# Start-up order, norm rows and value phases of a gated attention and spectral mix

## The chip, the cores and the metric

The kernel runs on one core of a Trainium2 chip. The metric is device time in microseconds for one execution: the median of three runs. One further execution is profiled, and its own time is given beside its span, which goes from the first to the last instruction.

## The reference

Two branches read the same kind of input and a sigmoid gate mixes them, row by row. Branch A is full attention with 16 heads of 28 columns over 2048 positions; branch B is a 2-D real Fourier transform, a multiplication by complex weights and the inverse transform.

```
g = sigmoid((A_x * gate_w).sum(-1))
qkv = (A_x @ wqkv)            # [2048, 448] @ [448, 1344]
p = softmax(q @ k.T * 28**-0.5)      # 16 heads, 2048 x 2048
a = (p @ v) @ wo
b = irfft2(rfft2(B_x) * (B_w_r + 1j * B_w_i))
return g * a + (1 - g) * b
```

In the kernel both branches read A_x.

## The kernel before

**Tiling.** The 16 heads form four groups of four heads; a head takes 32 rows (28 and some spare) of a 128-row tile, so that one group fills `q[g]` and `k[g]`, each [128, 2048]. Queries are taken in four blocks of 512. A *round* n is one group and one query block: 16 rounds. A round has 16 key tiles of 128 keys; a *unit* is one key tile and one head, 128 keys by 512 queries.

**Two ways of making exponentials.** For most units ScalarE makes them from PSUM: a *step* is three units (buffer `psA`, 1536 columns) or two (`psB`, 1024 columns) in turn, one instruction at L944, and the result goes to the SBUF ring. There are 331 steps. The last `ND[n]` key tiles of a round (49 in all) go another way: the score of one unit goes to a background bank `bg`, VectorE (L979, 196 times) adds a constant and writes it as a 16-bit integer whose bits are a rough exponential in bf16; then three more copies with shifted *phase* are made by VectorE or GpSimd (L990, 147 in all), each of 128x2048. The four phases are averaged by the accumulation: `vd[g]` holds the values multiplied by a weight for each phase.

**Norm rows.** The queries and keys have a spare row in each head with minus half the squared norm, which keeps the exponent in range. A row is made from squares (`sq`) and a small matmul with a constant (`cst`). `proj_group` (L690) makes it apart: project, evacuate to `k` or `q` (L710, L712), square (L716), matmul, evacuate to `nrow` (L731), and a DMA on SP's queue puts it into its rows. `proj_two` (L744), used for key block 1 of group 0, projects twice: once to get the squares, and once into a PSUM bank onto which the norm matmul then accumulates. The factor e^(..) that the key's norm takes away is put back by `w` (`w_block`, L776, exponentials at L806) into the values.

**Values.** `v_block` (L817) projects four key tiles' values into one bank; VectorE multiplies them by `w` into `vw` (L846), and for the last block of a group by four weights `wg` into the four phases of `vd` (L856), straight from PSUM.

**Head.** `head` (L496) starts the loads: x tiles and constants on SP's queue; on ScalarE's queue the query weights, the identity matrix, the key weights, in this order. Fourteen matmuls of zeros warm TensorE. x is transposed by TensorE into `psA`, `psB`, `pvb` and a background bank. Block 0 of the queries is projected twice (into `psA` for the squares, into `pvb` for the result with its norm row), and so are the first 128 keys; the other 384 keys of block 0 follow. `weights` loads the rest, `x_block` (L665) transposes the later x blocks.

**Spectral branch.** `background` gives the transforms as matmuls (`Bd`, `A`, `CS`, `Binv`) with DMA shuffles between them (`Ab`, `V2`), spread as background work over the whole kernel. `out_tile` adds both branches into PSUM (eight groups of matmuls for each of 16 row tiles).

**Order.** Every piece of work is an `Op` with an engine, a duration and dependences. The order in which they are issued is not worked out at run time: `PLAN` holds a list of op numbers, made beforehand, the background bank of each item, and the list of phases that VectorE rather than GpSimd makes. `issue` (L296) emits them in that order, and each engine runs its own instructions in order. Codes from 60000 in the list are fillers: small matmuls of zeros into the accumulator or a background bank. All matmuls in groups of four (one for each 32 rows or columns) come from L414, transposes from L422. Where a GpSimd op follows a VectorE op marked `lk`, `issue` adds a dependence between them.

```
for (n, kt, s) in st:
    deps += self.qev[g, c] + ([self.k0] if (g, kt) == (0, 0) else self.kev[g, kt // 4])
```

A score step waits for its queries (`qev`) and keys (`kev`; `k0` is the first 128 keys).

Of the kernel before, what the change touches and what calls it, by code (L numbers as in the profile page):

```python
# [39 lines left out]
TWO = (1,)  # L40
EARLY = 8
PLAN = (
    (
        'c-kFTW3XU7)0~-TCTDHiwr$(IYukF(wr$(CZQHtQd-uEF`y*9JD$}P=cPFV3SO9Pk6$Byxf`Vw^AtD429U_5-7!VE&M248q6=FdR'
        'V5kd~AU4#5dQc1EKz)b{wV@(3fOrrB%^*HBf(p<a8bbnT0pTGbG=Y|o2wFo2NDOVDBP4~kkOVqGJBR|QAUULj6wnz`Lr+K#-Jmk0'
        'fn?ANGC*4B4(T8>WP#q06?#B6$OwHP6ZC}wkR5WsK*$d{Ar}mT+>i(ILOv)6qoEKKh9Xb~N<&d71~VZom4#U_8`4p6C;=s*3Y3C!'
        'FbB%RTu4tDDFe-e`LF;M!VcI8yI>LQhD?;1_P}CT0!twa?S-tg4E8}b+7GMY0A#0wupCyvN>~FqXcer5LvR?@!4b$wM<Ewofva!~'
        'a?>@q4#(jp+=AP11M<)v$V+$O1mvUqbQ12teRu$;;2{*Cg7gR`Kp|QWkD)M4grc+oCczUZLK|T+td}Y96sE#7C`QkqI8BEcun9K9'
        '7T5|Us3dKJ?Qk0I*i!TrO4B#^4prd?oPn}bhR#AY_zCCWJZz8)@C(Y(MJP{~;4(aiyY@G{fQnRss>4h81EIhu_zFD!g-R4)9jHv<'
        'uqnKTH}Do3LKUh?@1Pa@gKG3106#!`s7@aNu?rC1v!5Uy)ubBq8SdK$_M!a(k8CY^Y!%j~{Su!Jh{l6*ND@#TN=S9-xIQdT>{DBh'  # L50
        'PUwifJ|&_^KC+ME6H^0fNKySW``jj>O%g&$sS#b!o8_Y3B3tE!ZA{yw34N3A@<W<ZGWsda=!{NIzvQJ2wJGSV-XqN^CAFZv^2(+n'
        'gDvT`ZAGc+ptiVAzS?j0kaoT`Ic!7Wk^LJhzAbs*j?U@8f44vEc^v`UQwNHOhxHNNk&fy}*oltmpZ1at2|X3oI#U<AtWRp~tm{g@'
        'Y&T+eU2e!t=}uR454t5+wQ)U3TravUzpZ!I^groMedx3f6WOOB@_os<esohSAGm(-$KKL^?SJ$i^r!3kt-Y=L!#jIJzqbQuAl=db'
        '>;Sl{2SG^a8Mzn6U@#1#!88QU3b_0FxqPrg=!FcWNBW$+l*c+$KH6av68cIW=;8ECf3oO4+vobcjGzlr*pH-(Qp8`9$oNo4!BJGy'
        'kEY8K6^r?3IEKg-_t9}IJ<(sRa!+*$9|L3JI11;+Q%N5SW8+YmKuKL34DTk=3!Tip)XCj&NZ}^Y2$)Robf}KuMnX*YUcc5U-4q%H'
        'Q|XN!1F76wJr+LbaWIXhQv~->f70V2qKoAsxz9R{n?Z4LCcV<}Fg||K32+w8roTENe$|m(Y?s<aadRlG`={s9PaW08aldplm(CrR'
        '6Ecs!>G||spOhc^lq{h1ZXul(W#YQ%P8(wu(PFYDp3CB$Swc%Gs~5v2gUjYaLcIwIO@xVY8D;m&DV#}yIebzK%nFL{R#Hx%48xoI'
# [188 lines left out]
class Kernel:  # L246
# [249 lines left out]
    def head(self):  # L496
# [9 lines left out]
        for i, (w, off) in enumerate((("q", 0), ("k", D))):  # L506
# [3 lines left out]
            if i == 0:  # L510
                d_id = self.dma(self.ident[:], ident.ap(), (), K0 + 1, eng="ACT", dur=0.43, lat=2.4)
# [52 lines left out]
        def proj(w, bank, a, b, last, key, deps=(), **it):  # L564
            ops = []
            for j, c in enumerate(CO):
# [5 lines left out]
                if it and it["first"] and ops:  # L572
                    d["first"] = False
# [769 lines left out]
```

## Time and profile before

| what | value |
|---|---|
| runs | 406.08 us median of 3 (405.11 to 407.94) |
| profiled execution | 405.44 us, span 403.6 us |
| TensorE (PE) busy | 390.3 us, 97%, 5099 matmuls |
| ScalarE (ACT) busy | 382.9 us, 95%, 350 instructions |
| VectorE (DVE) busy | 326.2 us, 81%, 527 |
| GpSimd (POOL) busy | 160.0 us, 40%, 190 |
| DMA | 21.69 MB, mean 54 GB/s |

Busy times are unions of instruction spans. Matmul spans overlap their successors and include their drain, so a TensorE that is 97% busy is not at its peak; where it matters the distance between starts is used. The first exponential starts at 12.34 us, the last at 392.70 us. In the timeline's rows the first number is the start in us, the second the duration in us (with x and a count: of the whole group), then engine, line, operation, output <- input and shape; in brackets the idle time of that engine just before, and what ended it. In rows that group instructions the numbers behind the bar are total busy time in us and mean time of one in ns, or min/median/max in ns.

### The profile page before, as it was taken

Reading aid. Unit: us, or ns where it says so; the run is one execution under the profiler, and the core shown is the slowest. Engines: PE = TensorE matmul, PEld = TensorE weight load, DVE = VectorE, ACT = ScalarE, POOL = GpSimd, SP = SyncE. Lnnn points to the kernel's source line nnn. Section 1 sums busy time; section 2 is a strip of 40 time slices with the busy share of each in tenths; the row PEclk is TensorE's granted clock in tenths of the full one; section 3 lists DMA queues with packets and bytes.
Section 4 is the critical chain, followed back from the end, with each engine's and each line's share of the span. In section 5 each row is a group of like instructions: output and inputs, shape, how many; then the busy total and the mean of one; then the engine's idle time right before and its main releaser. Section 6 shows DMA issues by size and latency. Waiting matters only on the chain.

```text
span 403.6 us, 12270 instructions
## 1 busy us (share of the span) xinstructions
PE 390.3 (97%) x5099; PEld 147.3 (36%) x5099; DVE 326.2 (81%) x527; ACT 382.9 (95%) x350; POOL 160.0 (40%) x190
## 2 busy tenths in 40 slices
PE   7999999999999999999999999899999999999996
PEld 5544333233343343323433333334333433333333
DVE  1456798997687999997899989899999998776733
ACT  3799999999989999999999999999999999999992
POOL 7004013531303332555345466561655557215230
PEclk9999999999999999999999999999999999999999
DMA  8014032220101011201222232323012201011011
GB/s 222 3 43 99 4 89 61 51 65 16 51 15 39 7 37 51 71 25 46 71 71 56 55 91 51 78 54 75 31 36 79 83 24 52 25 52 36 26 52 58
DMA packets 31995, 21.69 MB, mean 54 GB/s; under 512 B 16736, under 2 KB 29780, under 8 KB 31940
## 3 DMA queue, kind: packets, MB, share of 16 engines
q1 hardware_dynamic: 30580, 20.45, 18.8%
q8 instruction: 40, 0.66, 0.7%
q10 hardware_dynamic: 1360, 0.46, 0.4%
q14 instruction: 15, 0.12, 0.1%
HBM read 15.00 MB, written 1.97 MB: 42 GB/s over the span
## 4 chain that ended last, share of the span: by engine, by line
PE 65%; ACT 14%; DVE 11%; issue 5%; DMA 3%; POOL 2%; SPq 0%; ACTq 0%; DVEq 0%; POOLq 0%
PE bg L414 27%; PE pvb L414 19%; ACT ring L944 14%; PE psA L414 10%; PE psB L414 8%; DVE pd L979 4%; DVE pd L990 2%; POOL pd L990 2%; DMA ident<-cident 1%; DMA CS<-cCS 1%; DVE pvs L1058 1%; DVE X L1275 1%; DMA Rb<-rsc 1%; DVE tt L1232 1%; PE bg L422 1%
## 5 line engine op out<-in xcount | busy, mean ns | idle before, releaser
L944 ACT ACTIVATE ring<-psA 128x1536 bf16<-128x1536 f32 x162 | 247.6, 1529 | 1.6 <-PE psA L414 1.3
L944 ACT ACTIVATE ring<-psB 128x1024 bf16<-128x1024 f32 x161 | 178.3, 1107 | 3.3 <-PE psB L414 2.1
L979 DVE TENSOR_SCALAR pd<-bg 128x512 uint16<-128x512 f32 x196 | 130.0, 684 | 19.4 <-PE bg L414 17.1
L990 POOL TENSOR_SCALAR pd<-pd 128x2048 uint16<-128x2048 uint16 x56 | 105.6, 1897 | 90.5 <-DVE pd L990 31.1
L414 PEld LDWEIGHTS <-k 32*128 32x128 bf16 x1024 | 40.0, 91 | 111.7 <-issue 105.4
L414 PE MATMUL pvb<-ring,vw 128*32 128x512 bf16 x808 | 74.8, 384 | 0.3 <-DVE pvs L1058 0.3
L414 PE MATMUL bg<-q,k 32*128 32x512 bf16 x196 | 72.5, 381 | 0.5 <-DVE nrow L731 0.2
L414 PE MATMUL pvb<-pd,vd 128*32 128x512 bf16 x784 | 69.4, 384 | 1.8 <-DVE pvs L1058 0.8
L990 DVE TENSOR_SCALAR pd<-pd 128x2048 uint16<-128x2048 uint16 x91 | 69.5, 791 | 0.8
L414 PE MATMUL psA<-q,k 32*128 32x512 bf16 x498 | 65.8, 383 | 2.6 <-ACT ring L944 1.4
L414 PE MATMUL psB<-q,k 32*128 32x512 bf16 x330 | 66.8, 383 | 0.5 <-DVE k L613 0.2
L1069 POOL TENSOR_TENSOR q<-pvs,Rb 128x512 bf16<-128x512 f32 x15 | 19.6, 1304 | 41.8 <-DMA Rb<-rsc 32.1
L414 PEld LDWEIGHTS <-vw 128*32 128x32 bf16 x828 | 20.2, 94 | 33.9 <-issue 29.7
L414 PEld LDWEIGHTS <-vd 128*32 128x32 bf16 x784 | 20.3, 94 | 32.7 <-issue 26.9
L414 PEld LDWEIGHTS <-xT 112*128 112x128 bf16 (+1 forms) x512 | 18.9, 97 | 13.2 <-issue 10.3
L1062 POOL TENSOR_TENSOR rrg<-rr,G 128x16 f32<-128x16 f32 x15 | 3.3, 218 | 49.3 <-DVE rr L1061 37.7
L414 PE MATMUL bg<-xT,wpk 112*32 112x512 bf16 (+3 forms) x268 | 21.2, 380 | 0.1
L1232 DVE TENSOR_TENSOR tt<-bg,Wg 128x900 bf16<-128x900 f32 x16 | 17.4, 1093 | 2.9 <-PE bg L414 2.6
L414 PE MATMUL bg<-xT,wpq 112*32 112x512 bf16 (+1 forms) x240 | 18.0, 383 | 0.0
L414 PE MATMUL bg<-Bd,xT 112*32 112x450 bf16 x256 | 17.3, 357 | 0.0
L712 DVE TENSOR_SCALAR q<-bg 128x512 bf16<-128x512 f32 x15 | 10.3, 688 | 7.3 <-PE bg L414 7.3
L414 PE MATMUL pvb<-zero 128*32 128x256 bf16 x260 | 15.7, 276 | 0.2 <-DVE pvs L1058 0.2
(112 smaller groups left out, 341.9 us busy)
## 6 DMA issues: line engine op xcount, KB each, us to landing
Rb<-rsc SPq DMA_DIRECT2D x60, 64.0 KB
CS<-cCS SPq DMA_DIRECT2D x16, 192.0 KB
xtok<-Ab SPq DMA_DIRECT2D x16, 112.5 KB
Wg<-in_B_w_i_dram SPq DMA_DIRECT2D x64, 28.1 KB
V<-xtok SPq DMA_DIRECT2D x16, 112.5 KB
xtok<-in_A_x_dram SPq DMA_DIRECT2D x3, 448.0 KB
out_dram<-fin SPq DMA_DIRECT2D x12, 112.0 KB
Wg<-in_B_w_r_dram SPq DMA_DIRECT2D x32, 28.1 KB
```

What stands on the lines that cost most here:

```text
L414: self.pin(self.nc.tensor.matmul(out, lhsT=lhsT, rhs=rhs, start=start, stop=stop, **kw))
L422: self.pin(self.nc.tensor.transpose(out=out, in_=in_, identity=self.ident[0:n, 0:n]))
L712: self.pin(nc.vector.tensor_scalar(out=dst, in0=self.bgi(it), scalar1=CQ, scalar2=None, op0=ALU.mult))
L944: self.pin(nc.scalar.activation(out=home[:, u0:u0 + len(st), :], in_=slot[:, 0:len(st), :], func=ACT.Exp, scale=LN2 / UNITS))
L979: self.pin(nc.vector.tensor_scalar(out=self.pd[y.bank][:, s, :].bitcast(U16), in0=self.bgi(it), scalar1=127 * UNITS, scalar2=0.0, op0=ALU. ...
L990: self.pin(e.tensor_scalar(out=fl(self.pd[z.bank]), in0=fl(self.pd[y.bank]), scalar1=float(PHASE[f]), scalar2=1.0, op0=ALU.add, op1=ALU.mult))
L1058: ev = self.dve(0.6, lambda: self.pin(nc.vector.tensor_copy(out=pvs[:], in_=self.pv[:])), last + [self.nlast[i]], -1000.0, name="evac")
L1062: b = self.pool(0.2, lambda: self.pin(nc.gpsimd.tensor_tensor(out=rrg[:], in0=rr[:], in1=self.G4[:, c, :], op=ALU.mult)), [a] + self.g4d, ...
L1069: e = self.pool(1.24, lambda: self.pin(nc.gpsimd.tensor_tensor(out=dst, in0=pvs[:], in1=self.Rb[:], op=ALU.mult)), ds, kk)
L1232: self.pin(nc.vector.tensor_tensor(out=tt[:], in0=free_dims(self.bgi(it), [[0, 2], [F, 2], [1, F]]), in1=free_dims(Wg[:], [[F, 2], [F, 2], ...
L1275: self.pin(nc.vector.tensor_tensor(out=free_dims(self.zt[0:FN], [[128, 4], [1, 128]], 512 * t), in0=self.bgi(it)[0:FN, :].rearrange("p (a ...
```

## The change

- On ScalarE's queue the identity is loaded first, then the query weights, then the key weights.
- The start of group 0: the second query projection goes. VectorE scales the query from `psA` into `q`, a matmul puts the norm row alone into `pvb`, and VectorE adds the two. The first part of the keys is 256 instead of 128 columns (`KA`), and the squares of the rest are made by VectorE instead of ScalarE. The first half of x block 1 is transposed in the head; its second half uses `pvb`.
- `proj_add` takes the place of `proj_two` (key block 1) and of `proj_group` for the other blocks of group 0 (key blocks 2 and 3, query blocks 1 to 3): one projection, evacuated at once; its square; a matmul of the norm row into a second bank; and a VectorE instruction that adds it. The `nrow` copy and the DMA go.
- `v_block`: VectorE copies the values to a float tile `vraw`, and GpSimd makes the four phases of `vd` from it.
- Within a quad of the VectorE way, the four scores wait for the first score of the previous quad instead of its last.
- `w` has two buffers instead of four.
- A new `PLAN`: 2959 entries instead of 2964, 68 fillers instead of 66, 85 phases on VectorE instead of 91 (so 62 instead of 56 on GpSimd).

```diff
+KA = 256
...
             if i == 0:
-                d_id = self.dma(self.ident[:], ident.ap(), (), K0 + 1, eng="ACT", dur=0.43, lat=2.4)
+                d_id = self.dma(self.ident[:], ident.ap(), (), K0, eng="ACT", dur=0.43, lat=2.4)
+            raws[w] = self.dma(free_dims(self.U[0:C], [[C, 4], [1, C]], o), self.wsrc(off, 0, C), (), K0 + 1 + i,
+                               eng="ACT", dur=0.55, lat=3.0)
...
-        qb = proj("q", bqb, 0, 512, False, K0 + 22, [self.xev[0, 2], ka])
-        kb = proj("k", bkb, 0, 128, False, K0 + 23, [self.xev[0, 1], qb])
+        kb = proj("k", bkb, 0, KA, False, K0 + 22, [self.xev[0, 2], ka])
...
+        mq = self.pe(0.227, lambda: self.mm(bqb(), self.c("selq"), self.sq[:, 0:512], True, True),
+                     (sqq, self.d_cst, self.xev[0, 1]), K0 + 21)
...
+        qc = self.dve(0.6, lambda: self.pin(nc.vector.tensor_scalar(out=q0[:, 0:512], in0=bqa(), scalar1=CQ, scalar2=None,
+                                                                    op0=ALU.mult)), (qa, sqq), K0 + 50)
+        qe = self.dve(0.6, lambda: self.pin(nc.vector.scalar_tensor_tensor(
+            out=q0[:, 0:512], in0=bqb(), scalar=CQ, in1=q0[:, 0:512], op0=ALU.mult, op1=ALU.add)), (mq, qc), K0 + 51)
...
-    def proj_two(self, w, g, b, due):
+    def proj_add(self, w, g, b, due, rel=0.0):
...
+        e = self.dve(0.6, fe, ops[-1:], due - 4, it=it, rd=True, name="kqev")
+        q = self.dve(0.33, lambda: self.pin(nc.vector.tensor_tensor(out=s, in0=T, in1=T, op=ALU.mult)), [e] + self.sqrd,
+                     due - 4, lk=True, name="sq")
+        m = self.pe(0.217, lambda: self.mm4(self.bgi(it2), self.c("sel" + w), s, True, True), (q, self.d_cst), due - 3,
+                    mode="col", it=it2, first=True)
+        self.sqrd = [m]
+        z = 1.0 if w == "k" else 1.0 / CQ
+        (self.kev if w == "k" else self.qev)[g, b] = [self.dve(0.6, lambda: self.pin(nc.vector.scalar_tensor_tensor(
+            out=T, in0=self.bgi(it2), scalar=z, in1=T, op0=ALU.mult, op1=ALU.add)), (m, e), due - 3, it=it2, rd=True,
+            name="kqev")]
...
+            ev = self.dve(0.54, lambda: self.pin(nc.vector.tensor_copy(
+                out=self.vraw[:], in_=free_dims(self.bgi(it), [[m, 4], [1, C]]))), ops[-1:] + users, due - 1.4, it=it, rd=True)
+            users.clear()
             for f in range(4):
                 def fd(f=f):
-                    src = free_dims(self.bgi(it), [[m, 4], [DH, 4], [1, DH]])
+                    src = self.vraw[:].rearrange("p (k s j) -> p k s j", k=4, s=4)
                     wv = free_dims(self.wg[g][:], [[4, 4], [1, 4], [0, DH]], 16 * f)
-                    self.pin(nc.vector.tensor_tensor(out=self.vd[g][:, f, :, :, 0:DH], in0=src, in1=wv, op=ALU.mult))
-                o = self.dve(0.54, fd, [ops[-1], self.vdms[g], ("vwar", g), self.vdw[g][0]], due - 1.4, it=it, rd=True)
+                    self.pin(nc.gpsimd.tensor_tensor(out=self.vd[g][:, f, :, :, 0:DH], in0=src, in1=wv, op=ALU.mult))
+                o = self.pool(1.1, fd, [ev, self.vdms[g], ("vwar", g), self.vdw[g][0]], due - 1.4 + .3 * f)
...
-                    self.proj_group("k", 0, [b], due, 0.0)
+                self.proj_add("k", 0, b, due if b > 1 else -3000.0)
...
-            self.proj_group("q", 0, [b], ts[b] - 12.0, 0.0)
+            self.proj_add("q", 0, b, ts[b] - 9.0)
...
-                deps += self.qev[g, c] + ([self.k0] if (g, kt) == (0, 0) else self.kev[g, kt // 4])
+                deps += self.qev[g, c] + ([self.k0] if (g, kt * 128 // KA) == (0, 0) else self.kev[g, kt // 4])
...
-                m = self.pe(0.222, fm, self.kev[g, kt // 4] + self.qev[g, c] + [prevm] +
+                m = self.pe(0.222, fm, self.kev[g, kt // 4] + self.qev[g, c] + prevq +
...
-            prevm = ms[-1]
+            prevq = ms[:1]
```

More of the change, by code (lines that the diff above doesn't have):

```diff
@@ L667, in x_block @@
         for half in range(2):
-            it = Item()
+            own = (b, half) != (1, 1)
+            it = Item() if own else None
+            bank = (lambda it=it: self.bgi(it, BF16)) if own else (lambda: self.pv[:].bitcast(BF16))
             ops = []
```

271 lines of the change are left out of this document (130 added, 141 removed), and 17 rows, old and new, of the table PLAN.

## The prediction

> **What bounds the kernel now.** The span is cut in three with the windows view: before the first exponential, from it to the end of the last, and the tail. The columns are start:end, length, then busy time with instruction counts for PE, PEld, DVE, ACT and POOL.
>
> ```profile
> 0.00:12.34 12.34, 10.31 (x59) 6.64 (x60) 1.97 (x4) 4.25 (x9) 7.23 (x51) 1.00 0.68 183
> 12.34:394.20 381.86, 373.83 (x4918) 137.36 (x4922) 320.67 (x512) 377.01 (x340) 152.79 (x139) 1.00 0.19 49
> 394.20:403.60 9.40, 6.18 (x132) 3.27 (x120) 3.52 (x12) 1.60 (x3) 0.00 (x0) 0.95 0.19 63
> ```
>
> ScalarE and TensorE are both full in the middle. VectorE has 61 us to spare there, GpSimd 229. What the middle would take at ScalarE's own pace is read from the timeline where nothing is late:
>
> ```profile
> 379.13 1.51 ACT L944 ACTIVATE ring<-psA 128x1536 bf16<-128x1536 f32 x1
> 381.36 1.54 ACT L944 ACTIVATE ring<-psA 128x1536 bf16<-128x1536 f32 x1
> ```
>
> A pair (1536 and 1024 columns) takes 2.23 us. The kernel has 331 exponentials, 165.5 pairs, so 369 us, and some 2 us of other ScalarE work. About 10 us of the middle are therefore lost in gaps. The change doesn't touch the number or width of the exponentials, so it can win only the head, those gaps and the tail. The larger gaps carry the idle time in brackets:
>
> ```profile
> 12.34 1.45 ACT L944 ACTIVATE ring<-psA 128x1536 bf16<-128x1536 f32 x1
> 14.55 1.02 ACT L944 ACTIVATE ring<-psB 128x1024 bf16<-128x1024 f32 x1 [0.76 <-PE psA L414]
> 21.11 1.45 ACT L944 ACTIVATE ring<-psA 128x1536 bf16<-128x1536 f32 x1 [1.02 <-PE psA L414]
> 118.44 1.02 ACT L944 ACTIVATE ring<-psB 128x1024 bf16<-128x1024 f32 x1 [1.68 <-PE psB L414]
> ```
>
> Each waits for a score matmul. In front of that stands the evacuation of keys (14.55 and 21.11) or simply a long stretch of other TensorE work (118.44).
>
> **Part 1, the head.** The timeline of the first 12 us:
>
> ```profile
> 1.10 3.17 PE L414 MATMUL psA<-zero 128*128 128x256 bf16 x14 [1.10 <-POOL zero L514]
> 1.21 0.55 ACTq L397 DMA_DIRECT2D ident<-cident  x1
> 4.03 0.56 ACT L491 COPY wpq<-X 112x448 bf16<-112x448 bf16 x1 [0.25 <-DMA X<-in_A_wqkv_dram]
> 5.11 0.37 PE L422 MATMUL psA<-ident,xtok 128*113 128x128 bf16 x2 [0.83 <-DMA ident<-cident]
> 5.27 0.42 PE L422 MATMUL psB<-ident,xtok 128*113 128x128 bf16 x2
> 6.73 0.56 POOL L493 COPY wpk<-X 112x448 bf16<-112x448 bf16 x1 [1.67 <-DMA X<-in_A_wqkv_dram]
> 6.85 0.59 PE L414 MATMUL psA<-xT,wpq 112*128 112x512 bf16 x1
> 9.15 1.53 PE L414 MATMUL pvb<-xT,wpq 112*128 112x512 bf16 x4
> 9.39 0.60 ACT L580 ACTIVATE sq<-psA 128x512 bf16<-128x512 f32 x1 [0.58 <-PE psA L414]
> 11.02 0.81 PE L414 MATMUL bg<-xT,wpk 112*128 112x384 bf16 x4
> 11.16 0.69 DVE L606 TENSOR_SCALAR q<-pvb 128x512 bf16<-128x512 f32 x1 [3.05 <-PE pvb L414]
> 11.90 0.39 PE L414 MATMUL psA<-q,k 32*128 32x512 bf16 x3
> ```
>
> The ACT queue lands its three transfers one after the other: query weights by 4.03, identity by 5.11, key weights by 6.73. With the identity first, the transposes can start when the 14 warm-up matmuls end (4.27). The query weights take the identity's old place, about 5.05, and their copy ends at 5.6. Eight transpose pairs at 0.21 end at 5.9. The query projection starts at 5.65 instead of 6.85 and isn't interrupted: 4 x 0.43 gives 7.4. The copy wpk ends at 7.29, as now, just in time.
>
> Then, at the slow rate of 0.43 per 512 columns (the granted clock is 1.00 in the windows above, so it is not the throttle that these rows show): key projection of 256 columns 0.85 (8.25); half of its second copy 0.43, the query's norm row 0.43 (its square, 0.60 after 7.4, is ready), the other half 0.43, the key's row 0.21, so 9.75. The second query projection (the 1.53 us row) is gone: VectorE scales the query from psA meanwhile, and adds the row by 9.85. The ScalarE copy of 256 key columns is about 0.4 (10.2). TensorE's order puts eight transposes and one projection first (0.85 and 0.2), the scores at 10.8, the exponential 0.44 later as now: 11.25. If the fast rate comes by 7.9, the same walk with halved matmuls, VectorE's 0.69 us evacuations now setting its end, gives 9.9; the 384-column row above ran at it (four before the next start at 11.67, 0.16 each). I take 10.6, between the two: **-1.7 us** (-2.4 to -1.1; -0.8 if the identity lands no earlier).
>
> The Trainium skill, "TensorE: Matmul & The Clock Gate" (Part 1: The HAM clock gate), says that full clock comes after about 3.4 us of sustained activity in a free-running window. By that rule the unbroken run of matmuls from 1.10 would be fast by 7.9, the first exponential at 9.9, and the sum 0.7 lower; the trace agrees in that the 3.17 us run at 1.10 was followed by slow transposes.
>
> **Part 2, the first key blocks.** 256 key columns ready at once make eight units, so the first three steps need nothing else and the 0.76 gap goes; the rest of block 0 is made under those three exponentials. Next late is key block 1, wanted by the seventh exponential, now at 21.11, 8.77 after the first against 3 x 2.23 = 6.7.
>
> ```profile
> 18.42 0.68 DVE L681 COPY xT<-bg 113x1024 bf16<-113x1024 bf16 x1
> 19.02 0.41 DVE L762 TENSOR_TENSOR sq<-sq 128x512 bf16<-128x512 bf16 x1
> 19.49 0.40 PE L414 MATMUL bg<-sq,cst 128*32 128x512 bf16 x4
> 19.93 0.69 DVE L770 CAST k<-bg 128x512 bf16<-128x512 f32 x1 [0.50 <-PE bg L414]
> 20.47 0.60 PE L414 MATMUL psA<-q,k 32*128 32x512 bf16 x3
> ```
>
> In the new order VectorE has, after the block's projection, copy 0.69, square 0.41, two transposed x blocks (0.68 each), and then the addition of the row. In-order TensorE finishes that projection behind the fifth step, about 4.4 us after the first exponential; 0.69 + 0.41 + 1.36 + 0.69 and hand-overs make the block ready near 7.6, the exponential at 8.05. **-0.7 us** (-2.0 if the x copies fall into gaps, +0.5 if they come a step later).
>
> The other norm rows of group 0 cost VectorE the same as before:
>
> ```profile
> L731 DVE CAST nrow<-bg 32x512 bf16<-32x512 f32 x5 | 3.4, 672 | 2.2 <-PE bg L414 2.2
> L846 DVE TENSOR_TENSOR vw<-bg,w 128x448 bf16<-128x448 f32 x13 | 8.0, 618 | 3.0 <-PE bg L414 3.0
> L1232 DVE TENSOR_TENSOR tt<-bg,Wg 128x900 bf16<-128x900 f32 x16 | 17.4, 1093 | 2.9 <-PE bg L414 2.6
> L856 DVE TENSOR_TENSOR vd<-bg,wg 128x448 bf16<-128x448 f32 x16 | 8.9, 616 | 0.0
> ```
>
> An addition of a PSUM tile and an SBUF tile isn't in the trace; the two-operand rows beside it are 0.62 (448) and 1.09 (900), so about 0.69 at 512, against 0.67 for the nrow copy that goes. Five row DMAs leave SP's queue, each a wait that held everything behind it. For key block 1 four projection groups vanish (0.9 us of TensorE). All this lies under the exponentials: 0 here, and +0.7 for each block whose addition comes last.
>
> **Part 3, the order table.** The 1.68 gap at 118.44 hides no wait of TensorE: between the scores of psA at 114.71 and the next, of psB, stand 13 groups of matmuls, seven of value projections (first row) and six accumulations:
>
> ```profile
> 115.04 1.55 PE L414 MATMUL bg<-wvr,xT 112*128 112x112 bf16 x28
> 116.03 2.21 DVE L856 TENSOR_TENSOR vd<-bg,wg 128x448 bf16<-128x448 f32 x4
> 117.93 0.39 PE L414 MATMUL psB<-q,k 32*128 32x512 bf16 x2
> ```
>
> After the start-up the new order has at most eight groups between scores, some 1.8 us at 0.22 each (0.16 x 512/384), less than the 2.23 of a pair that two score buffers cover. **-1.3 us** (-1.7 to 0: the total of TensorE's work stays, so some of it may be late elsewhere).
>
> **Part 4, GpSimd.** Sixteen value phases (616 ns each, 9.9 us) leave VectorE, four copies of about 0.62 come: -7.4 us. Counted in the order, VectorE makes 85 phases instead of 91: -4.1.
>
> ```profile
> L990 POOL TENSOR_SCALAR pd<-pd 128x2048 uint16<-128x2048 uint16 x56 | 105.6, 1897 | 90.5 <-DVE pd L990 31.1 <-DVE pd L979 25.6 <-DMA wo<-in_A_wo_dram 18.0
> L990 DVE TENSOR_SCALAR pd<-pd x91: 631/685/2012, 55.5 to 385.0; 128x2048 uint16<-128x2048 uint16 x91
> L1069 POOL TENSOR_TENSOR q<-pvs,Rb 128x512 bf16<-128x512 f32 x15 | 19.6, 1304 | 41.8 <-DMA Rb<-rsc 32.1 <-DVE pd L990 9.8
> ```
>
> GpSimd gains 6 x 1.9 and 16 x 1.14 (448/512 of the two-input row L1069): 160 becomes 190 us of 403, still half idle. The place to watch is head group 1: its first value phase is issued after score step 107 and read by an accumulation right after step 109. Copy 0.62 and two phases 2.3 make 2.9 us, against 2.2 to 3.0; a 1.9 us phase stands between the second and the third. In-order TensorE stands behind whichever is late, scores included. **+0.5 us** (-0.3 if VectorE's relief shows, +2 if all four are late). Groups 0, 2 and 3 have 3 to 35 steps of slack.
>
> **Part 5, the tail.** Behind the last score stand 35 groups instead of 40. Output groups take 0.19 each:
>
> ```profile
> 398.68 0.95 PE L414 MATMUL bg<-Bd,X 113*32 113x448 bf16 x16
> 399.44 0.94 PE L414 MATMUL bg<-wo,q 128*32 128x448 bf16 x16
> ```
>
> (0.76 for four), so -0.95, of which I let half return as later scores: **-0.5 us** (-0.95 to +0.5). The freer key order within a quad and the shared w buffers, whose readers ended long before: nothing.
>
> **Sum.** -1.7 - 0.7 - 1.3 + 0.5 - 0.5 = -3.7. The profiled execution took 405.44 (span 403.6 and 1.84 around it), 0.64 under the median 406.08 of runs between 405.11 and 407.94. 405.44 - 3.7 = **401.7 us**.
>
> **The rivals.** (a) *TensorE eats the gain.* It is 373.83 busy of 381.86 in the middle and its work there hardly shrinks. If it, not ScalarE, sets the end, the gap at 118.44 only moves, and head and tail alone arrive: 405.44 - 1.7 - 0.5 = 403.2, up to 406 if the identity lands no earlier either. For it: the gaps all wait for TensorE. Against: fillers that compute nothing are in its order, so it has slack.
>
> ```profile
> L414 PE MATMUL pvb<-zero 128*32 128x256 bf16 x260 | 15.7, 276 | 0.2 <-DVE pvs L1058 0.2
> ```
>
> (b) *GpSimd holds VectorE up: slower.* The VectorE phase has a median of 685 but a maximum of 2012 ns: a collision with GpSimd costs 1.33 us, and its mean of 791 by
>
> ```profile
> L990 DVE TENSOR_SCALAR pd<-pd 128x2048 uint16<-128x2048 uint16 x91 | 69.5, 791 | 0.8
> ```
>
> shows 9.6 us lost so already. The 22 new long GpSimd instructions could cost VectorE 22 x 1.33 = 29 us, and each late phase stops TensorE at its accumulation. From seven exposed collisions on (9.3 us against 4.2 of gain) the kernel is over 1% slower: about 411, worse with more. Against: VectorE gets 11.5 us back.
> The Trainium skill, "SBUF — State Buffer" (SBUF: two separate sides), calls the shared port pair an exclusive lock held for a whole instruction; by that rule this rival is the kernel's own mechanism, and the 2012 ns agree.
>
> (c) *More falls than I count.* The fast rate comes early, key block 1 is in time, and the many gaps of 0.1 to 0.3 shrink with VectorE's relief: -2.4 - 2.0 - 1.7 - 1 = -7.1, 398.
>
> **How the numbers follow.** About 1% (4.1 us) is what a measurement of this kernel can tell from no change. Forecast 0.52 (of it 0.42 beyond 1%, since 402.0 is the bound), (a) 0.20, all within, (b) 0.16, (c) 0.12. So faster 0.54, same 0.30, slower 0.16. The range is 398 to 408: it holds the forecast's own 399.5 to 404 and (a), and leaves out half of (b) and a part of (c).
>
> **What would show it.** First exponential at 9.9 to 11.3, the transposes at about 4.2 and the copy wpq near 5.05; second exponential directly behind the first; seventh about 8 us after the first; no idle over 0.8 in the middle except around the steps of group 1's value phases; GpSimd near 190 us, VectorE near 315; the last exponential's end to the span's end below 9.4. It is wrong if the middle stays at 382 or more, or if VectorE's phases average over 900 ns.

## The result and the profile after

The kernel after takes 401.12 us (median of 4 runs, 400.41 to 401.43); the kernel before, run beside it, 405.69 us. The ratio is 0.9875 with a 95% interval of 0.9834 to 0.9915. The forecast was 401.7 us. The profiled execution took 400.41 us with a span of 398.6, against 405.44 and 403.6.

The windows view of the kernel after, cut as before (ahead of the first exponential, from it to the end of the last, the tail); columns are start:end, length, then busy time with counts for PE, PEld, DVE, ACT, POOL:

```profile
0.00:9.53 9.53, 8.09 (x58) 5.52 (x58) 2.96 (x6) 3.90 (x8) 7.17 (x51) 1.00 0.77 220
9.53:389.93 380.40, 370.38 (x4938) 138.63 (x4938) 313.71 (x496) 377.08 (x339) 179.37 (x161) 1.00 0.19 50
389.93:398.60 8.67, 5.38 (x113) 3.42 (x106) 3.20 (x11) 1.50 (x3) 0.00 (x0) 0.94 0.17 55
```

The span is 5.0 us shorter. Of this 2.81 lie in the head (12.34 to 9.53), 1.46 in the middle (381.86 to 380.40), 0.73 in the tail (9.40 to 8.67). The timeline of the head, after (in this view and the later ones rows in between are left out):

```profile
4.06 0.42 PE L422 MATMUL psA<-ident,xtok 128*113 128x128 bf16 x2
...
5.00 0.57 ACT L491 COPY wpq<-X 112x448 bf16<-112x448 bf16 x1 [1.29 <-DMA X<-in_A_wqkv_dram]
...
5.73 1.14 PE L414 MATMUL psA<-xT,wpq 112*128 112x512 bf16 x4
6.39 0.56 POOL L493 COPY wpk<-X 112x448 bf16<-112x448 bf16 x1 [1.27 <-DMA X<-in_A_wqkv_dram]
7.00 0.61 PE L414 MATMUL bg<-xT,wpk 112*128 112x256 bf16 x4
8.35 0.69 DVE L607 SCALAR_TENSOR_TENSOR q<-pvb,q 128x512 bf16<-128x512 f32 x1
9.09 0.39 PE L414 MATMUL psA<-q,k 32*128 32x512 bf16 x3
9.53 1.45 ACT L955 ACTIVATE ring<-psA 128x1536 bf16<-128x1536 f32 x1 [0.73 <-PE psA L414]
10.87 1.02 ACT L955 ACTIVATE ring<-psB 128x1024 bf16<-128x1024 f32 x1
...
17.49 1.45 ACT L955 ACTIVATE ring<-psA 128x1536 bf16<-128x1536 f32 x1 [1.08 <-PE psA L414]
```

Read it from the top. The transposes start in the order of the new queue, at 4.06. Four query matmuls of 512 columns take 1.14 us together: TensorE is already at its fast rate at 5.73. The packed trace holds the moments at which the granted clock changed; its first entry, the step to full clock, stands at 5.01 here. Ahead of the first entry the windows view prints 1.00 as well, although the matmuls are still slow. The second exponential stands directly behind the first; the seventh, at 17.49, still waits 1.08.

To see where ScalarE loses time in the middle, take the distance between starts, less 1.34 us after a three-unit exponential and 0.91 after a two-unit one, and add up what is left. Before that sum is 9.11 us, after 7.65. Up to the seventh exponential the distance fell from 8.77 to 7.96. Of the rest, 0.65 us shorter, the 1.88 lost before 118.44 are the largest piece: at the same steps 0.57 is lost now, but 0.52 has come at 39.28 (the first rows below) and 0.64 at 237.88 (the last). Other gaps changed too: the 0.59 before 39.50 and the 0.69 and 0.40 before 257.19 and 258.50 (TensorE waited 1.07 us there for the load of CS) are all but gone, and 0.45 before 342.85 and 0.35 before 374.88 are new. The 0.65 is what many such changes leave. From the timeline after:

```profile
37.71 0.85 DVE L883 TENSOR_SCALAR gg<-gg 128x16 bf16<-128x16 bf16 x1
38.62 0.23 PE L414 MATMUL bg<-ident,gg 128*32 128x128 bf16 x1 [0.45 <-DVE gg L883]
...
39.28 1.45 ACT L955 ACTIVATE ring<-psA 128x1536 bf16<-128x1536 f32 x1 [0.39 <-PE psA L414]
...
236.88 0.57 PE L414 MATMUL bg<-Z,CS 128*32 128x450 bf16 x12 [0.43 <-POOL Z L1249]
...
237.88 1.45 ACT L955 ACTIVATE ring<-psA 128x1536 bf16<-128x1536 f32 x1 [0.48 <-PE bg L414]
```

Both have the same form: a matmul of a side branch waits for its operand, and in-order TensorE keeps the scores behind it.

### The profile page after: what moved, and what is told of

Same layout as the page of the kernel before. It is cut to its first block, busy times and chain, and to the rows that moved or that the text cites. A ratio compares the mean times of both kernels' runs of the same rounds, so it can differ in the third digit from the quotient of the medians.

```text
span 398.6 us, 12284 instructions
## 1 busy us (share of the span) xinstructions
PE 383.9 (96%) x5102; PEld 147.6 (37%) x5102; DVE 319.9 (80%) x512; ACT 382.5 (96%) x349; POOL 186.5 (47%) x212
## 4 chain that ended last, share of the span: by engine, by line
PE 63%; ACT 19%; DVE 8%; issue 6%; POOL 1%; DMA 1%; ACTq 0%; DVEq 0%; POOLq 0%
PE bg L414 25%; PE pvb L414 19%; ACT ring L955 18%; PE psA L414 9%; PE psB L414 9%; DVE pd L990 3%; DVE pd L1001 2%; DMA X<-in_A_wqkv_dram 1%; POOL pd L1001 1%; ACT pd L955 1%; DVE tt L1243 1%; DVE pvs L1069 0%; PE bg L422 0%; DVE xT L689 0%; DVE k L769 0%
## 5 line engine op out<-in xcount | busy, mean ns | idle before, releaser
L955 ACT ACTIVATE ring<-psA 128x1536 bf16<-128x1536 f32 x162 | 243.8, 1505 | 4.0 <-PE psA L414 2.5
L955 ACT ACTIVATE ring<-psB 128x1024 bf16<-128x1024 f32 x161 | 174.6, 1085 | 0.0
L1001 POOL TENSOR_SCALAR pd<-pd 128x2048 uint16<-128x2048 uint16 x62 | 117.5, 1904 | 109.2 <-DVE pd L1001 46.4
L414 PE MATMUL bg<-q,k 32*128 32x512 bf16 x196 | 71.4, 382 | 0.2
L1001 DVE TENSOR_SCALAR pd<-pd 128x2048 uint16<-128x2048 uint16 x85 | 66.7, 806 | 1.4
L414 PEld LDWEIGHTS <-xT 112*128 112x128 bf16 (+1 forms) x512 | 19.0, 97 | 13.9 <-issue 11.5
L414 PE MATMUL bg<-xT,wpk 112*32 112x512 bf16 (+2 forms) x252 | 19.3, 378 | 0.5 <-DVE xT L689 0.2
L868 POOL TENSOR_TENSOR vd<-vraw,wg 128x448 bf16<-128x448 f32 x16 | 14.7, 941 | 5.6 <-DVE pd L1001 2.2
L1149 DVE CAST fin<-bg 128x448 bf16<-128x448 f32 x12 | 7.4, 619 | 10.4 <-PE bg L414 10.4
```

The lines of the kernel that those rows point to most:

```text
L414: self.pin(self.nc.tensor.matmul(out, lhsT=lhsT, rhs=rhs, start=start, stop=stop, **kw))
L868: self.pin(nc.gpsimd.tensor_tensor(out=self.vd[g][:, f, :, :, 0:DH], in0=src, in1=wv, op=ALU.mult))
L955: self.pin(nc.scalar.activation(out=home[:, u0:u0 + len(st), :], in_=slot[:, 0:len(st), :], func=ACT.Exp, scale=LN2 / UNITS))
L1001: self.pin(e.tensor_scalar(out=fl(self.pd[z.bank]), in0=fl(self.pd[y.bank]), scalar1=float(PHASE[f]), scalar2=1.0, op0=ALU.add, op1=ALU.mult))
L1149: e = self.dve(0.55, lambda: self.pin(nc.vector.tensor_copy(out=fin, in_=bank())), [ops[-1], self.fdma[t % 2]], key, **a)
```

## The experiments

In the tables below, "middle" is the distance from the start of the first exponential to the start of the last (380.36 before, 378.90 after), so that the head doesn't disturb it. Ratios are against the kernel before, run on the same chip.

### The head: start or rate

**Identity first in the kernel before.**

```diff
+            if i == 0:
+                d_id = self.dma(self.ident[:], ident.ap(), (), K0 + 1, eng="ACT", dur=0.43, lat=2.4)
             raws[w] = self.dma(...)
-            if i == 0:
-                d_id = self.dma(self.ident[:], ident.ap(), (), K0 + 1, eng="ACT", dur=0.43, lat=2.4)
```

> The kernel before with one part of the change alone: on ScalarE's queue the identity is loaded ahead of the query weights. Two theories for the 2.81 us by which the first exponential came earlier after the change. Theory 'start': the gain is the earlier start of the transposes (5.11 to 4.1) and the second query projection that went; then this part alone brings the first exponential from 12.34 to about 11.3 and the run 1.0 us. Theory 'rate': with the identity early the run of matmuls from 1.10 isn't interrupted, TensorE runs at the fast rate from about 5 us instead of 10.3, and every matmul of the head takes half; then this part alone brings the first exponential to 9.6 to 10.2 and the run about 2.4 us, nearly all of the head's gain.

**Four more warm-up matmuls in the kernel before**, so that TensorE works until the identity lands.

```diff
-            warm.append(self.pe(0.213, lambda: self.mm(...), (ms0,), K0 + i * .01))
+            warm.append(self.pe(0.213, lambda i=i: [self.mm(...) for _ in range(5 if i == 13 else 1)], ...))
```

> The kernel before, identity second as before, with 18 instead of 14 warm-up matmuls of zeros, so that they end at about 5.1 us, where the transposes start, instead of 4.27: no gap. Theory 'start': nothing is gained, the first exponential stays at 12.3. Theory 'rate': the fast rate comes at about 5 us and the first exponential at 10.3 to 10.8; 1.5 to 2 us gained without touching any transfer.

**Identity second in the kernel after**: the two loads in the old order, all else new.

> The changed kernel with the query weights ahead of the identity again, everything else as changed. Theory 'start': the transposes start 1.0 us later and so does the first exponential: 10.5; plus 1.0 us. Theory 'rate': the gap after the warm-up is back, the head runs at the slow rate, the first exponential comes at 11.3 to 12; plus 1.8 to 2.5 us.

**Warm-up matmuls of 128 instead of 256 columns in the kernel after.**

```diff
-self.mm(self.slots[0][:, 0, 0:256], self.zero[:, 0:P], self.zero[:], True,
+self.mm(self.slots[0][:, 0, 0:128], self.zero[:, 0:P], self.zero[:, 0:P], True,
```

> The changed kernel with warm-up matmuls of 128 instead of 256 columns, so that they end at about 2.7 us and TensorE is idle until the transposes at 4.06. Theory 'start': the transposes, projections and the first exponential stay where they are (9.5). Theory 'rate': the fast rate comes later by 2 us or more and the first exponential at 10.6 to 11.3; plus 1.1 to 1.8 us.

| kernel | first exponential | us, median | ratio (95%) |
|---|---|---|---|
| before, identity first | 10.99 | 404.0 | 0.9974 (0.9959 to 0.9988) |
| before, longer warm-up | 11.16 | 404.87 | 0.9986 (0.9967 to 1.0005) |
| after, identity second | 10.16 | 401.52 | 0.9906 (0.9875 to 0.9937) |
| after, half warm-up | 11.02 | 402.09 | 0.9914 (0.9892 to 0.9936) |

The rows that decide. From the timeline of the kernel before with identity first:

```profile
7.01 0.56 POOL L493 COPY wpk<-X 112x448 bf16<-112x448 bf16 x1 [1.95 <-DMA X<-in_A_wqkv_dram]
8.30 1.03 PE L414 MATMUL pvb<-xT,wpq 112*128 112x512 bf16 x4
```

From that with the longer warm-up:

```profile
5.24 0.37 PE L422 MATMUL psA<-ident,xtok 128*113 128x128 bf16 x2
8.47 1.03 PE L414 MATMUL pvb<-xT,wpq 112*128 112x512 bf16 x4
```

From the kernel after with identity second:

```profile
5.24 0.27 PE L422 MATMUL psA<-ident,xtok 128*113 128x128 bf16 x2 [0.98 <-DMA ident<-cident]
```

And from the kernel after with half the warm-up:

```profile
6.00 1.91 PE L414 MATMUL psA<-xT,wpq 112*128 112x512 bf16 x4
11.02 1.45 ACT L955 ACTIVATE ring<-psA 128x1536 bf16<-128x1536 f32 x1 [0.52 <-PE psA L414]
```

Each part counts, and no one theory explains all. Identity first is worth about 1 us alone (10.99 against 12.34 in the kernel before and 12.12 as the median of three profiles with the old head; 1.2 us of time). The rate is worth as much: with half the warm-up the query matmuls start nearly as early (6.00), but four of them take 1.91 instead of 1.14, and the first exponential comes 1.49 later than in the profiled kernel after (1.16 later than the median of six profiles with the new head). The longer warm-up in the kernel before brings the fast rate too, from 7.00 and with the old start (its time can't be told from no change). Against the third kernel, whose transposes start at the same 5.24, its first exponential is 1.0 later: 0.6 of it because its transposes were still slow (first query matmul at 6.98 against 6.37), the rest with the old start-up's second query projection (the 1.03 us rows) and its order, which these runs don't part. In the third kernel TensorE idled 0.98 us and its next transposes were fast all the same, 0.11 apart: its first clock entry stands at 4.51, inside that idle time.

The clock entries tell what decides the moment. Two kernels further below have a stretch at half clock in the middle of the run; it lasts 3.41 us in both, and every stretch at full clock that lies between two entries is a whole multiple of this (392.53 us is 115 times 3.413). So take the piece of 3.41 us that ends at the first entry, and the piece before it. In all fourteen profiles TensorE is idle for at most 0.35 us in the last piece, and for 0.84 us or more in the one before (the time ahead of the first matmul at 1.10 counts as idle). Where the pieces lie differs from execution to execution, and this makes the head vary. With the identity early TensorE is busy from 1.10 on almost without a break, and the six profiles of the new head change at 5.01, 5.04, 5.13, 6.02, 6.18 and 6.48. With the old head the break that starts at 4.27 falls into a piece and spoils it; the three profiles change at 8.66, 9.16 and 10.15. The third kernel has that break too, but in its one profile a piece ran from 1.10 to 4.51 and held only 0.24 us of it. So its 10.16 is a lucky draw, and what identity second costs in the new head isn't settled by it. The half warm-up is one draw as well, change at 9.78: TensorE is busy from 3.73 on but for 0.27 us, so an estimate from these pieces allows any change from 7.1 on. That it costs is seen in the time too: its four runs, 401.61 to 402.39, all lie above the four of the kernel after.

**Key weights on another queue.** One more edit of the head was run, in a kernel that also has the three moved matmuls of the next section.

```diff
-                               eng="ACT", dur=0.55, lat=3.0)
+                               eng=("ACT", "SP")[i], dur=0.55, lat=3.0)
```

> The kernel of the three moved matmuls with one more edit: the first key weights are loaded on SP's queue, directly behind the first two x tiles, instead of third on ScalarE's queue. In the kernels with the new head their copy wpk began between 5.80 and 7.07 us and the first exponential between 9.53 and 10.05. Theory 'key weights' (with fast matmuls their landing is what the key projection waits for): copy wpk near 5.5, no wait of TensorE in front of the key projection, first exponential 9.2 to 9.5, total 0.4 lower than without (399.9). Theory 'rate' (the time of the fast rate sets it): first exponential 9.6 to 10.1 whatever the landing, total 400.3. Theory 'queue' (the constants and x tiles behind it on SP's queue come 0.5 later and the norm rows or block 1 wait for them): first or seventh exponential later by 0.3 or more.

It took 400.01 us, ratio 0.9868 (0.9841 to 0.9894). Its timeline:

```profile
5.24 0.47 PE L430 MATMUL psA<-ident,xtok 128*113 128x128 bf16 x2 [0.33 <-DMA xtok<-in_A_x_dram]
5.65 0.56 POOL L501 COPY wpk<-X 112x448 bf16<-112x448 bf16 x1 [0.54 <-DMA X<-in_A_wqkv_dram]
6.35 1.33 PE L422 MATMUL psA<-xT,wpq 112*128 112x512 bf16 x4
10.34 1.45 ACT L963 ACTIVATE ring<-psA 128x1536 bf16<-128x1536 f32 x1 [0.85 <-PE psA L422]
```

The key weights were early, but the second x tile landed late (5.24), the query matmuls began late, and their first was still slow (the clock entry is at 6.96). The first exponential, 10.34, lies outside what any of the theories gave, nearest to 'rate'. Neither of the other two is settled by it. The same x tile was waited for until 5.08 and 5.42 in two kernels without this edit, so its lateness can't be laid to the fuller queue, as 'queue' would have it. And the time, 400.01, can't be told from the 400.27 of the kernel with the three moves alone.

### The gap at 118.44

**Two scores moved ahead in the kernel before**, those of steps 89 and 90, into the stretch of value projections.

```diff
+        move(733, 338)
+        move(735, 1856)
```

> The kernel before with two score steps moved in its order and nothing else: of the 13 groups of matmuls that stood between two scores near 115 us, three now stand ahead of the first moved score, five between it and the second, the rest behind. Theory 'gap': a gap of ScalarE is a real loss, since ScalarE sets the pace; the 1.88 us at 118.44 go, the last exponential starts at about 391.0 instead of 392.7, and the run is 1.5 us shorter. Theory 'TensorE': its work in the middle sets the end; the gap comes back in pieces over the next 50 steps, and the last exponential stays within 0.5 us of 392.7.

It took 405.84 us, ratio 1.0012 (0.9992 to 1.0033); the middle is 1.91 longer. Its timeline around the place:

```profile
118.51 1.45 ACT L951 ACTIVATE ring<-psA 128x1536 bf16<-128x1536 f32 x1 [0.79 <-PE pvb L421]
...
120.99 1.02 ACT L951 ACTIVATE ring<-psB 128x1024 bf16<-128x1024 f32 x1 [1.03 <-PE bg L421]
```

The 1.88 us lost once are now lost as 0.96 and 1.14. The theory 'gap' falls: TensorE has more to do in this stretch than its scores' distance allows, and moving the scores only moves the wait. (Another 0.9 of the lengthening is a later wait of an accumulation for a GpSimd phase, 0.99 at 290.72. The kernel with the longer warm-up, whose order is that of before, waits 0.74 at the same accumulation, so this part isn't shown to come from the moves.) What the new table did beside this, taking work out of the stretch, was not tried by itself.

**Three matmuls moved in the kernel after**: the gate's transposition behind the late evacuation, and a pair of the spectral branch (`Z`, `CS`).

```diff
+        move(538, 1756)
+        move(2735, 1511)
+        move(2736, 1511)
```

> The kernel after with three matmuls moved in the order: the gate's transposition behind the evacuation that was late (0.39 us of idle before the exponential at 39.28), and a pair of the spectral branch ahead (0.48 at 237.88). Nothing else. Theory 'gap' (what ScalarE waits there comes off the end): 400.0, 0.9 to 1.2 below the kernel after. Theory 'TensorE' (the work in between stays and the wait comes back at a later step, as at the scores of steps 89 and 90 in the kernel before): 400.8 to 401.5.

It took 400.27 us, ratio 0.9889 (0.9863 to 0.9914). Its timeline at the two places, and ten steps behind the second:

```profile
39.07 1.47 ACT L963 ACTIVATE ring<-psA 128x1536 bf16<-128x1536 f32 x1
...
237.14 1.49 ACT L963 ACTIVATE ring<-psA 128x1536 bf16<-128x1536 f32 x1
...
239.73 1.45 ACT L963 ACTIVATE ring<-psA 128x1536 bf16<-128x1536 f32 x1 [0.18 <-PE bg L422]
...
248.96 1.45 ACT L963 ACTIVATE ring<-psA 128x1536 bf16<-128x1536 f32 x1
```

Both gaps are gone (1.16 us in the distances between starts). The first doesn't come back: up to 237.14 nothing of it is lost again. The second comes back nearly whole, 0.35 two steps later (239.73) and 0.23 ten steps later (248.96). In the end the middle is 0.51 shorter. The two other kernels that hold these moves (key weights on another queue, and the next one) show the same gaps gone and the same ones come. So one gap was kept whole and of the other next to nothing. In the time this can't be told from the kernel after.

**These three moves, and key block 1 earlier.** Its norm row goes into `pvb`, its addition stands ahead of the two x copies, and the scores of the seventh exponential ahead of the next projection.

```diff
+        move(167, 206)
+        move(168, 187)
+        move(560, 188)
...
+        row = (lambda: self.pv[:]) if (w, b) == ("k", 1) else (lambda: self.bgi(it2))
```

> The changed kernel with three waits taken out of TensorE's order. The norm row of key block 1 goes to pvb, which is free then, instead of a background bank that still holds x, its addition comes ahead of two x copies, and the seventh step's scores ahead of the next projection; the gate's matmul and one spectral matmul pair come behind a score step instead of ahead. Theory 'gap': the gaps at 17.49 (1.24), 39.28 (0.52) and 237.88 (0.64) shrink by 0.7, 0.4 and 0.5, and the run is 1.3 to 1.6 us shorter. Theory 'TensorE': only the first, at the start, counts; 0.3 to 0.7 us shorter, the rest comes back elsewhere.

It took 401.03 us, ratio 0.9886 (0.9867 to 0.9904). The seventh exponential comes 7.36 after the first, 0.6 earlier than in the kernel after, but what was put off is missed at once; its timeline:

```profile
17.39 1.45 ACT L967 ACTIVATE ring<-psA 128x1536 bf16<-128x1536 f32 x1 [0.48 <-PE psA L425]
...
19.57 1.02 ACT L967 ACTIVATE ring<-psB 128x1024 bf16<-128x1024 f32 x1 [0.72 <-PE psB L425]
```

The 21st exponential stands 25.33 after the first, against 24.63 in the kernel after. So this one exchange doesn't better the start-up; others were not tried.

### GpSimd and VectorE

**Value phases back on VectorE in the kernel after**, straight from PSUM at the place of the copy; the order table stays.

```diff
-            ev = self.dve(0.54, lambda: self.pin(nc.vector.tensor_copy(out=self.vraw[:], in_=...
+            ev = self.dve(0.54, direct, ops[-1:] + users, due - 1.4, it=it, rd=True)
```

(`direct` holds the four products that L856 made before. GpSimd's four operations keep their places in the table and do nothing.)

> The changed kernel with the value phases made by VectorE straight from PSUM, four in a row where the float copy stood; GpSimd makes none, the order is otherwise the same. Theory 'relief': the 7.4 us that VectorE saved were worth something; the middle gets 1 us or more longer. Theory 'lock': GpSimd's phases held VectorE up (the 16-column instruction L883 took 850 ns while three of them ran, and the exponential at 39.28 came 0.4 us late); without them that gap goes and the run is 0.3 to 0.6 us shorter. Theory 'hidden': both lie under the exponentials; within 0.3 us.

**Part 4 alone in the kernel before**, with two `w` buffers to make room for `vraw`; the first two phases are issued together.

```diff
+            ev = self.dve(0.54, raw, dep, due - 1.4, it=it, rd=True)
+            o1 = self.pool(2.0, lambda: [fd(0), fd(1)], [ev], due - 1.4)
+            o2 = self.pool(1.0, lambda: fd(2), [ev], due - 1.4)
+            o3 = self.pool(1.0, lambda: fd(3), [ev], due - 1.4)
```

(`raw` copies the bank to `vraw`, `fd` is GpSimd's product.)

> The kernel before with Part 4 alone: VectorE copies the values to a float tile, GpSimd makes the four phases (the first two together, behind one another), w has two buffers so that the tile finds room; the order table stays that of before. Theory 'relief' (the value phases are a burden on VectorE wherever they stand, 2.2 us in one piece at each of four places): 401 to 403.5, VectorE busy near 319. Theory 'table' (taking them back in the kernel after cost 5.9 only because the new table had been laid out for a VectorE free at those places): 404.5 to 406.5, no difference from before. Theory 'lock' (an accumulation stands right behind the phases and meets the slower GpSimd): 408 or more, with TensorE waiting for the value phases at the steps of group 1.

**Twelve more phases on GpSimd in the kernel after** (74 instead of 62).

```diff
-        for i in alts:
+        for i in [i for j, i in enumerate(alts) if j % 7 != 3]:
```

> The changed kernel with 12 of VectorE's 85 phases, every seventh, made by GpSimd instead, in the same order (62 to 74 on GpSimd, 23 us more of it). Rival (b) of the prediction: a GpSimd phase that runs beside VectorE's holds it up and its late result stops TensorE; 12 x 1.2 us of later results, of which a third shows: plus 3 to 8 us. Theory 'slack': GpSimd is half idle and the accumulations come steps later; within 0.5 us.

**Six fewer phases on GpSimd in the kernel after** (56).

```diff
-        for i in alts:
+        rest = [i for i, o in enumerate(self.ops) if o.alt and i not in alts]
+        for i in list(alts) + rest[5::10]:
```

> The kernel after with 6 of the 62 phases taken back from GpSimd to VectorE (56 on GpSimd as before the change, 91 on VectorE), spread evenly, each at its place in the table. Twelve more on GpSimd had cost 9 us. Theory 'lock' (what costs is each GpSimd phase beside VectorE): 399.5 to 400.7. Theory 'balance' (both engines have dates that bind, and the split of the table is near the best): 402 to 404. Theory 'slack' (neither binds at this split): 400.8 to 401.6.

| kernel | us, median | ratio (95%) | middle against its parent |
|---|---|---|---|
| after, value phases on VectorE | 407.06 | 1.0029 (0.9998 to 1.0061) | +5.97 |
| before, value phases on GpSimd | 408.58 | 1.0086 (1.0058 to 1.0113) | +3.75 |
| after, 12 more on GpSimd | 410.1 | 1.0125 (1.0072 to 1.0178) | +7.59 |
| after, 6 fewer on GpSimd | 402.09 | 0.9927 (0.9905 to 0.995) | +1.46 |

All four have a longer middle. In time the first three are clearly slower than their parents; the interval of the last overlaps that of the kernel after (0.9834 to 0.9915). The wait view says where (its columns: us in total, times, longest). With the value phases back on VectorE:

```profile
PE bg L414 <- DVE vd L865: 4.8, 4, 1.6
```

The timeline of this kernel at one of the four places:

```profile
171.19 2.21 DVE L865 TENSOR_TENSOR vd<-bg,wg 128x448 bf16<-128x448 f32 x4
...
173.45 0.37 PE L414 MATMUL bg<-q,k 32*128 32x512 bf16 x1 [1.58 <-DVE vd L865]
...
175.12 1.45 ACT L959 ACTIVATE ring<-psA 128x1536 bf16<-128x1536 f32 x1 [1.43 <-PE bg L414]
```

Four products hold VectorE and the background bank for 2.2 us; the matmul that wants a bank waits, the scores stand behind it, ScalarE idles. In the kernel after the copy of 0.6 us frees bank and engine. The stall costs more than itself. The windows view behind it (columns as in the result; the figure that follows POOL's count is the granted clock):

```profile
172.29:175.70 3.41, 2.25 (x25) 0.70 (x24) 3.41 (x7) 1.98 (x3) 0.00 (x0) 1.00 0.24 73
175.70:179.11 3.41, 3.41 (x30) 1.71 (x27) 2.42 (x5) 2.85 (x3) 0.00 (x0) 0.50 0.00 0
```

The piece of 3.41 us with the stall has 1.16 us of idle TensorE, and in the next the granted clock is halved: TensorE starts 30 matmuls in it, against 56 in the one behind it, and ScalarE loses another 0.67 and 0.31 before the exponentials at 178.05 and 180.71. Over the ten runs of this kernel the time goes with the mean granted clock: 405.5 and 405.8 us at 1.00, 408.1 to 408.6 at 0.991 to 0.994.

Now Part 4 in the kernel before, its timeline at the one place that costs:

```profile
272.75 1.02 POOL L1243 TENSOR_TENSOR Z<-tt 128x225 bf16<-128x225 bf16 x1
273.73 0.94 POOL L856 TENSOR_TENSOR vd<-vraw,wg 128x448 bf16<-128x448 f32 x1
274.63 0.56 POOL L1245 TENSOR_TENSOR Z<-tt 128x225 bf16<-128x225 bf16 x1
275.24 0.94 PE L415 MATMUL bg<-Z,CS 128*32 128x450 bf16 x12 [2.43 <-POOL Z L1245]
...
277.05 1.45 ACT L951 ACTIVATE ring<-psA 128x1536 bf16<-128x1536 f32 x1 [2.75 <-PE psA L415]
```

VectorE's 5.5 us of relief brought nothing; a small GpSimd instruction of the spectral branch, queued behind the value phases, came 2.43 late and cost 2.9 us, most of the loss. Here too the granted clock reads 0.50 behind it, from 274.90 to 278.31, and the matmuls between 275.24 and the next scores are slow for it. 'Relief' falls, and 'lock' was right about a loss but not about the reader: no accumulation waited there. So the new table and the value phases on GpSimd are one piece: the table without them loses all that the head gains, and they are a loss without the table. (This holds for the two tables as they are; one made anew for VectorE's products was not tried.) The wait view of the kernel with twelve more phases on GpSimd:

```profile
PE pvb L414 <- POOL pd L1001: 5.7, 8, 1.1
```

Its groups (total in us, mean in ns):

```profile
L1001 DVE TENSOR_SCALAR pd<-pd 128x2048 uint16<-128x2048 uint16 x73 | 63.4, 886 | 1.6
```

Its timeline where it loses most:

```profile
240.28 0.40 PE L414 MATMUL pvb<-pd,vd 128*32 128x512 bf16 x4 [0.95 <-POOL pd L1001]
241.16 1.89 POOL L1001 TENSOR_SCALAR pd<-pd 128x2048 uint16<-128x2048 uint16 x1
241.24 0.57 PE L414 MATMUL bg<-Z,CS 128*32 128x450 bf16 x12 [0.57 <-POOL Z L1249]
...
242.24 1.45 ACT L955 ACTIVATE ring<-psA 128x1536 bf16<-128x1536 f32 x1 [1.80 <-PE bg L414]
```

Eight accumulations wait 5.7 us for GpSimd's phases, though GpSimd is busy only 52% of the span. Six fewer on GpSimd lose less, 1.46 in the middle, and 0.37 of it stands already at the seventh exponential, ahead of the first phase, where an x tile landed late. So more phases on GpSimd are clearly worse; that fewer are worse too rests on 1.1 us in one profile.

## Why the prediction was right, and where not

**Sum.** Forecast -3.7 to 401.7; the runs differ by 4.6 in the median and the two profiled executions by 5.0. The head term carries the difference of 1.3 between 5.0 and 3.7 nearly alone (1.1).

**Part 1, -1.7; measured -2.81 in this pair.** The moves were as told (wpq at 5.00, transposes at 4.06, first exponential's inputs in the order walked through). The step that failed is the choice of 10.6 "between the two": the fast rate was there at 5.01. The pair overstates it by luck, since the head varies, and it sets the latest change of the clock with the old head (10.15) against the earliest with the new (5.01): three profiles with the old head (before and two of the experiments) have the first exponential at 12.34, 12.12 and 11.71, six with the new one at 9.53, 9.65, 9.85, 9.86, 10.03 and 10.05. The medians, 12.12 and 9.86, give -2.26, inside the stated -2.4 to -1.1 but near its end. The case with the fast rate, 9.9, was the one to take. By the window of about 3.4 us that the Trainium skill, "TensorE: Matmul & The Clock Gate" (Part 1: The HAM clock gate), gives, the estimate was fast by 7.9 in the new head; the trace agrees, the six turned fast between 5.01 and 6.48, and the half warm-up, at 9.78, fits a rule that counts activity.

**Part 2, -0.7; measured -0.81.** The seventh exponential came 7.96 after the first (8.05 forecast), for the reason given: the gap before the second exponential went (0.87 by the distances), and the seventh is waited for as long as before (1.24 against 1.16). The timeline after shows the two x copies of VectorE ahead of the row's addition (its matmul waits for the first of them only), and the addition at the price of a 0.69 row:

```profile
15.13 1.28 DVE L689 COPY xT<-bg 113x1024 bf16<-113x1024 bf16 x2
15.86 0.40 PE L414 MATMUL bg<-sq,cst 128*32 128x512 bf16 x4 [0.36 <-DVE xT L689]
16.33 0.68 DVE L779 SCALAR_TENSOR_TENSOR k<-bg,k 128x512 bf16<-128x512 f32 x1
```

**Part 3, -1.3, and Part 4, +0.5: together -0.8; measured -0.65.** The sum is right, the two terms are not two, and that it came so near is luck in part. At 118.44 about 1.3 fell, as forecast; 1.6 more fell before 39.50, 257.19 and 258.50, which the forecast didn't name, and 2.2 returned elsewhere. The step that failed is that I took the table's gain and GpSimd's cost for addends. Taking Part 4 out costs 5.97, and putting it in alone costs 3.75. Three of the four places were free of stalls, group 1's, the one to watch, among them; at group 0's the products held up the gate's small VectorE instruction, and that is the 0.52 at 39.28 (see rival (b)). VectorE's relief was 6.3 us (326.2 to 319.9) instead of 11.5: the copies and phases gave 9.3 of it, and the rest of the new work took 3.0 back (the seven additions 4.8, against 3.4 that went with the five nrow copies, and smaller pieces). The value phase on GpSimd took 0.94 instead of the 1.14 estimated from the q row, by one tile's view:

```profile
L868 POOL TENSOR_TENSOR vd<-vraw,wg x16: 939/942/943, 35.8 to 279.9; 128x448 bf16<-128x448 f32 x16
```

**Part 5, -0.5; measured -0.73** (9.40 to 8.67), with 19 fewer TensorE instructions in the tail. From the last exponential's start to the end it is 10.2 in all nine profiles with the new table, and 10.9 in all five with the old: this term belongs to the table and repeats.

**The rivals.** (a) TensorE eats the gain: true where a gap came back (the second of the two that were moved aside, and the one at 118.44 in the kernel before), not in the whole. (b) GpSimd holds VectorE up: not at this load, since the VectorE phases went only from 791 to 806 ns; at 74 phases it is real (886 ns, +7.59 us), mainly because readers wait for GpSimd's own phases. A tiny VectorE instruction shows the hold-up plainly: the gate's took 850 ns beside the value phases, ended with GpSimd's third product (38.56 and 38.54) and cost 0.4. With the products on VectorE it takes 172 ns, and the groups of the kernel before have it at 161:

```profile
L870 DVE TENSOR_SCALAR gg<-gg 128x16 bf16<-128x16 bf16 x1 | 0.2, 161 | 0.0
```

The Trainium skill, "SBUF — State Buffer" (SBUF: two separate sides), has this as an exclusive lock; the 850 ns agree, but a price by collisions alone missed where the loss arises. (c) Fast rate early: that part of it came, the others not.

## What to carry to other kernels

Price an order table and the assignment of work to engines together: each was a loss without the other. On an in-order engine that is nearly full, moving a late instruction aside kept all of one gap and next to nothing of another, and moving the waiting one ahead of a full stretch recovered nothing: look ten steps on before you count a gap as won. Spend the first microseconds on keeping TensorE dense: half the warm-up cost over 1 us of the head in its profile and 1.0 us in the median of the runs. Later, a long stall of TensorE can cost more than itself: behind the two longest in the middle of a run the clock was halved for 3.41 us.

## What was not expected of the hardware

- When TensorE turned fast differed between executions of the same instruction stream: between 5.01 and 6.48 us in six profiles with the new head, between 8.66 and 10.15 in three with the old. The first exponentials spread over 0.5 and 0.6 us beside it, with a share of late loads in that. All fourteen first changes fit pieces of 3.41 us that start at another moment in each execution and must be nearly free of idle time: 0.35 us was still allowed, 0.84 no longer.
- In the middle of a run, TensorE's idle 1.58 us (with the value phases on VectorE) and 2.43 us (Part 4 alone) were each followed by 3.41 us at half the granted clock. A wait of 1.55 us for the load of CS (Part 4 alone, until 255.83) had no such stretch behind it, so the length of the wait alone doesn't decide; what does stays open.
- The three loads on ScalarE's queue landed at varying times: with identity first, the copy of the key weights began between 5.80 and 6.92 us in kernels with the same head, the last TensorE waiting up to 0.48 for it.
- A GpSimd product of 448 float columns took 0.94 us, against 1.30 for the 512 columns of the q row: less than in proportion.
